# A linear-attention query stage: small softmax steps moved to GpSimd, turned halves in their own slot, and a Strassen sum moved from SBUF to PSUM

## The chip, the cores and the metric

The kernel runs on one core of a Trainium2 chip. The metric is the device time of one execution in microseconds. Three executions took 1721.21 to 1723.33 us, median 1722.93; the profile was taken in another one. The engines are called as in the profile: PE (TensorE, matmul), PEld (its weight loads), DVE (VectorE), ACT (ScalarE), POOL (GpSimd) and SP (SyncE, which issues all DMAs here).

## The reference

Two attention layers with their own inputs are computed, and their outputs stand side by side. Both have 2048 tokens, a width of 1024 and 32 heads of 32.

```python
# A: softmax attention in 4 segments of 512 tokens, with a memory carried from one to the next
q, k, v = x @ wq, x @ wk, x @ wv                  # per head
p = softmax(q k^T * scale + mask)                 # inside a segment
o = g * (phi(q) M) / (phi(q) z) + (1 - g) * p v   # then M += phi(k)^T v, z += sum phi(k)
a = o @ wo

# B: linear attention with a learned feature map per head
q, k, v = x @ wqkv
phi(t) = [softmax(t w_phi), softmax(-t w_phi)]    # 64 features a head
kv = phi(k)^T v ;  z = sum_s phi(k)
o = (phi(q) kv) / (phi(q) z + 1e-6)
b = o @ wo
return concat([a, b])
```

## The kernel before

**Products.** All large products are fp16 with split operands: a number is held as a high and a low half, and each product is three matmuls (high by high, high by low, low by high) that are summed in a PSUM bank. The products of B's tokens with their weights, and A's output product, are Strassen-Winograd products: for a pair of token tiles (256 tokens) seven half products of 12 matmuls each give four outputs of 128 tokens by 512 columns. `strassen` keeps three of the running sums in SBUF (`p1`, `u2`, `p5`, tag `cs` with four buffers). Three of its four outputs come to stand in PSUM banks (DVE adds a kept sum to a bank in place, line 620). The fourth, output (1, 1), is the sum `p5`, which DVE writes back into its SBUF buffer: `add(p5, X, p5)`. The argument `kinds` names the PSUM banks of a product. There are eight banks; the planner grants at most three of kind `proj`, three `s`, two `misc`, one `pv` and four `kv` at a time.

**Stages.** To about 900 us: A's attention, by 32 units of a segment and four heads, with the preparation of B's weights and tokens beside it. Then B's value and key products to about 1210 us: for eight token pairs, keys go through the double softmax and phi(k)^T v is summed (`kv`). Then the query stage to about 1574 us, and last A's output product.

**The query stage**, where most of the change lies, runs over 16 token tiles `c`; each even `c` makes the Strassen product of a pair. Each of the four outputs goes to `expo`: DVE takes the maxima and minima of each head (`mx`, line 1264), subtracts (`e`, lines 1266 and 1268), ACT takes the exponentials (1271), DVE sums them (1274) and takes the reciprocal (`r`, 1277). Then, for each tile and half of the heads (`hb`), 32 turns in all:

1. POOL multiplies `e` with the key sums `zb` (line 1579, two halves), DVE sums the result to `dn` (1582);
2. DVE makes the factor of each softmax, four small steps: `dn` times `r` (1585), the two sums plus 1e-6 (1587), the reciprocal (1589), and `r` times that times 2^14 (1590);
3. POOL multiplies `e` with that factor (1592);
4. ACT writes the high half (1601), DVE the low half (1603), both into a buffer `eh` that is drawn from the same ring `e` of five buffers as the softmaxes themselves;
5. SP issues a transposing DMA to `pt` (1606), PE multiplies `pt` with `kls`, phi(k)^T v (`pv`, 1615), ACT and DVE split the result into `ot` (1619, 1621), and `project` multiplies it with B's `wo` (`misc`, 396).

Beside it the weights of A's output product are made, seven Strassen forms of four blocks each (`weights`): ACT writes the high half (508), POOL the low one (509). Three forms (B11, B21, T1) stay in SBUF slots S8, S13 and S12; four go through buffers `cs` to DRAM (`wo_d`) and are loaded back into slots S0 to S3 near the end (1568).

**What sets the order.** Every step is recorded with an estimated duration and a priority, and a planner (`Graph.run`) lists them engine by engine: it takes the ready step with the earliest start, and among those the lowest priority. The order on each engine is then fixed, and on the chip each waits in its queue for the semaphores of the steps it needs. A table `MOVES` adds an offset to the priority of single jobs of an engine, by the job's number. A changed duration, engine or bank so also moves other steps.

Of the kernel before, what the change touches and what calls it, by code (L numbers as in the profile page):

```python
# [8 lines left out]
F32 = mybir.dt.float32  # L9
F32R = mybir.dt.float32r  # L10
F16 = mybir.dt.float16
# [7 lines left out]
S = 2048  # L19
# [37 lines left out]
MOVES = {  # L57
# [6 lines left out]
    "DVE": {  # L64
# [4 lines left out]
    "ACT": {  # L69
# [3 lines left out]
    "POOL": {  # L73
        59: 0.5, 67: 5.5, 70: -0.5, 93: -6, 141: 5, 154: -8, 173: 3, 199: 12, 202: -3, 211: -16.5, 234: -5.5, 238: -29.5,
        250: -2, 252: 1.5, 257: 0.5, 312: -11.5, 326: -7},
    "SP": {
        88: 5, 89: 2.5, 107: -2.5, 131: 3, 134: 21.5, 183: 8, 184: -7, 223: 6.5, 226: -9, 238: -37},
# [204 lines left out]
def tile_kernel(ctx: ExitStack, tc: tile.TileContext, ax, aw, awv, awo, beta, bx, bwqk, bwv, bphi, bwo, out):  # L282
# [10 lines left out]
    wo_d = dram.tile([4, 128, 2, 4, 512], F16, name="wo_d")  # L293
# [308 lines left out]
    def strassen(x, w, prio, kinds, tag, out):  # L602

        X, Y, Z = (bank(k, [128, 512]) for k in kinds)
# [14 lines left out]
        def add(t, ps, o):  # L619
            op(DVE, 0.62, lambda: nc.vector.tensor_tensor(o(), t(), ps(), op=OP.add), r=[t, ps], w=[o], prio=prio)  # L620

# [10 lines left out]
        add(p5, X, p5)  # L632
        out(1, 1, p5)
# [689 lines left out]
    for n, p in enumerate(VT + (0,)):  # L1323
# [9 lines left out]
        strassen(x, wvf, L + 0.5, ("proj", "proj", "proj"), ("a", [128, 512], F32, "pk", 2), vout(p, vs, L + 0.5, keep_v if p else None))  # L1333
# [36 lines left out]
    KB = ("proj", "misc", "s")  # L1370
    for at_, p in enumerate(SEQ):
# [14 lines left out]
        if at_ not in VFIRST:  # L1386
            strassen(x, wkf, P, KB if p else ("proj",) * 3, CS, kout)
# [115 lines left out]
    wform = {}  # L1503
    ast = G.buf("b", [128, 16], F32, "ast", 1)
# [20 lines left out]
    SECOND, wob = ("T2", "T3", "B22", "T4"), G.fixed(wo_d)  # L1525
# [20 lines left out]
    for c in range(NT):  # L1546
        P = Q0 + c
        if c % 2 == 0:
            sk, er = times(c // 2, 0, P - 1.2), {}

            def qout(i, hb, ps, er=er, sk=sk, P=P):
                er[i, hb] = expo(ps, P, sk)

            strassen(x, wqf, P - 1.2, ("proj", "proj", "proj"), CS, qout)
            if c + 2 < NT:
                x = x1 if c == 0 else xkept(c // 2 + 1, XS, P)
        ot = G.buf("b", [128, 2112], F16, "ot", 4)
# [16 lines left out]
        for hb in range(2):  # L1574
            e, r = er[c % 2, hb]
            dn = G.buf("b", [128, 16, 2], F32, "dn", 2)
            for a in range(2):
# [7 lines left out]
            op(DVE, 0.1, lambda dn=dn, r=r: nc.vector.tensor_tensor(dn(), dn(), r(), op=OP.mult),  # L1585
               r=[dn, r], w=[dn], prio=P)
            op(DVE, 0.1, lambda dn=dn, d1=d1: nc.vector.scalar_tensor_tensor(
                d1(), dn()[:, :, 0], 1e-6, dn()[:, :, 1], op0=OP.add, op1=OP.add), r=[dn], w=[d1], prio=P)
            op(DVE, 0.15, lambda d1=d1: nc.vector.reciprocal(d1(), d1()), r=[d1], w=[d1], prio=P)
            op(DVE, 0.1, lambda d1=d1, r=r: nc.vector.scalar_tensor_tensor(  # L1590
                r(), r(), 2.0 ** 14, d1()[:, :, None].to_broadcast([128, 16, 2]), op0=OP.mult, op1=OP.mult), r=[d1, r], w=[r], prio=P)
# [3 lines left out]
            eh = G.buf("b", [128, 16, 2, 32], F32, "e", 5)  # L1595

            def hv(eh=eh):
                return eh().rearrange("p h s d -> p (h s d)").bitcast(F16).rearrange("p (a n) -> p a n", a=2)

            for q in range(2):  # L1600
                op(ACT, 0.53, lambda q=q, e=e, hv=hv: nc.scalar.activation(  # L1601
                    hv()[:, 0, 512 * q:512 * q + 512], ev(e)[:, 512 * q:512 * q + 512], AF.Copy), r=[e], w=[(eh, (0, q))], prio=P)
                op(DVE, 0.7, lambda q=q, e=e, hv=hv: nc.vector.tensor_tensor(  # L1603
                    hv()[:, 1, 512 * q:512 * q + 512], ev(e)[:, 512 * q:512 * q + 512], hv()[:, 0, 512 * q:512 * q + 512], op=OP.subtract),
                   r=[e, (eh, (0, q))], w=[(eh, (1, q))], prio=P, port=True)
# [135 lines left out]
```

## Time and profile before

| | |
|---|---|
| median of three executions | 1722.93 us (1721.21 to 1723.33) |
| profiled execution | 1722.68 us |
| its span, first to last instruction | 1721.0 us |
| granted PE clock over the span | 0.992 |
| attention, to about 900 us | PE 887 of 900 us busy |
| values and keys, 900 to 1210 us | PE 307 of 310, DVE 245, ACT 200, POOL 182 |
| queries, 1210 to 1574 us | PE 334 of 364, DVE 334, ACT 167, POOL 212 |
| A's output, 1574 to 1721 us | PE 143 of 147, DVE 60 |

All times are of one profiled execution, in microseconds unless marked ns. A group's row has the source line, the engine, the operation, output and inputs by the program's names, their shapes and the count; behind the bar the busy time, the mean of one in ns, and behind the second bar the idle time of the engine just before them, with what ended it. A wait's row names the engine and line that waited, the work that released it, the sum, the number of times and the longest. A row of a single line has the shortest, median and longest duration in ns. Tile names come without their numbers, so `e` in a group is any buffer of that tag.

### The profile page before, as it was taken

How to read it: one execution, taken by the hardware profiler on the slowest of the kernel's cores; microseconds unless marked ns; L12 is line 12 of the kernel's file. 1: busy time of each engine (PE TensorE's matmuls, PEld its weight loads, DVE VectorE, ACT ScalarE, POOL GpSimd, SP SyncE). 2: the span in 40 equal slices, each digit the busy share in tenths (PEclk: the TensorE clock that was granted, in tenths of full speed). 3: DMA queues.
4: the chain of work that ended last, by engine and by line, in shares of the span. 5: the costliest groups of instructions: out<-in, count | busy, mean ns of one | idle time of the engine just before them, and what ended most of it. 6: DMA issues, size and time to landing. Idle time of an engine off the chain costs nothing.

```text
span 1721.0 us, 38652 instructions
## 1 busy us (share of the span) xinstructions
PE 1670.3 (97%) x14408; PEld 1002.9 (58%) x14408; DVE 1408.9 (82%) x3269; ACT 1159.6 (67%) x2131; POOL 955.2 (56%) x1184
## 2 busy tenths in 40 slices
PE   8999999999999999999999999999799899999999
PEld 6667677676776776677755545455344444444444
DVE  6999999899998767797885889778999999987441
ACT  8788999888888978678854676665445554345331
POOL 3346588653668775756742678645656767440000
PEclk9999999999999999999999999999989999999999
DMA  6556456666666573764467464566456565646311
GB/s 211 162 167 185 155 186 190 216 182 184 196 188 204 148 217 94 203 192 115 150 189 258 148 215 135 177 220 251 156 125 149 127 175 128 196 107 198 121 67 61
DMA packets 260699, 290.37 MB, mean 169 GB/s; under 512 B 138784, under 2 KB 191776, under 8 KB 253984
## 3 DMA queue, kind: packets, MB, share of 16 engines
q1 hardware_dynamic: 260512, 287.91, 55.7%
q8 instruction: 113, 1.85, 0.5%
q14 instruction: 74, 0.61, 0.1%
HBM read 160.12 MB, written 85.00 MB: 142 GB/s over the span
## 4 chain that ended last, share of the span: by engine, by line
PE 45%; DVE 15%; DMA 2%; ACT 2%; issue 1%; POOL 1%; SPq 0%; DVEq 0%; ACTq 0%; POOLq 0%
PE proj L610 14%; PE proj L396 8%; PE proj L1669 5%; PE s L610 3%; PE misc L396 3%; DVE e L1603 3%; PE s L1669 2%; DMA pt<-e 2%; PE misc L610 2%; DVE mx L1264 2%; DVE r L1274 1%; DVE dn L1582 1%; PE pv L1009 1%; PE s L973 1%; PE misc L1669 1%
## 5 line engine op out<-in xcount | busy, mean ns | idle before, releaser
L396 PE MATMUL proj<-S,S 128*128 128x128 f16 (+1 forms) x3072 | 504.6, 300 | 4.8 <-DVE S L431 1.8
L396 PEld LDWEIGHTS <-S 128*128 128x128 f16 x4608 | 329.7, 98 | 150.7 <-issue 9.3
L610 PE MATMUL proj<-S,S 128*128 128x512 f16 x1584 | 368.4, 381 | 8.3 <-ACT cs L616 6.1
L610 PEld LDWEIGHTS <-S 128*128 128x128 f16 x2016 | 191.9, 98 | 226.1 <-issue 12.8
L986 POOL TENSOR_SCALAR_AFFINE_SELECT ph<-ph 128x256 f16<-128x256 f16 (+1 forms) x448 | 194.3, 456 | 165.5 <-DVE ph L980 147.9
L878 DVE CUSTOM_DVE_ANT_0 s<-s,causal 128x256 f32<-128x256 f32 (+3 forms) x512 | 242.9, 508 | 14.1 <-PE s L872 10.8
L980 DVE SCALAR_TENSOR_TENSOR ph<-s,ph 128x512 f16<-128x512 f32 x320 | 211.0, 684 | 51.6 <-ACT ph L979 50.2
L979 ACT ACTIVATE ph<-s 128x512 f16<-128x512 f32 x320 | 191.5, 659 | 0.8
L396 PE MATMUL misc<-S,ot 128*128 128x512 f16 x768 | 172.5, 382 | 1.1 <-ACT ot L1619 1.1
L1271 ACT ACTIVATE e<-e,sk 128x256 f32<-128x256 f32 x256 | 113.8, 497 | 55.3 <-DVE e L1268 46.1
L396 PEld LDWEIGHTS <-ot 128*128 128x128 f16 x768 | 74.2, 98 | 90.8 <-issue 2.2
L1579 POOL TENSOR_TENSOR e<-e,zb 128x512 f32<-128x512 f32 x64 | 86.1, 1369 | 56.5 <-DVE r L1274 45.4
L973 PE MATMUL s<-S 104*128 104x512 f16 (+3 forms) x512 | 114.7, 299 | 0.9 <-DVE mu L951 0.5
L872 PE MATMUL s<-S 96*128 96x512 f16 (+3 forms) x512 | 113.2, 299 | 0.8 <-DVE mt L878 0.4
L977 ACT ACTIVATE s<-s,os 128x512 f32<-128x512 f32 x160 | 106.2, 714 | 9.5 <-PE s L973 6.8
L977 ACT ACTIVATE s<-s,bd 128x512 f32<-128x512 f32 x160 | 106.8, 712 | 5.5 <-PE s L973 4.8
L396 PE MATMUL proj<-wv,S 128*128 128x128 f16 x1536 | 104.9, 219 | 0.1
L1601 ACT ACTIVATE e<-e 128x512 f16<-128x512 f32 x64 | 37.3, 622 | 97.0 <-POOL e L1592 47.5
L1009 PEld LDWEIGHTS <-ph 128*128 128x128 f16 x2560 | 87.3, 96 | 17.7 <-issue 1.4
L1009 PE MATMUL pv<-vl,ph 128*128 128x66 f16 (+1 forms) x2560 | 92.2, 184 | 0.8 <-DVE h L826 0.3
L1274 DVE TENSOR_REDUCE r<-e 128x32 f32<-128x1024 f32 x64 | 76.6, 1207 | 12.5 <-ACT e L1271 12.4
L1592 POOL TENSOR_TENSOR e<-e,r 128x1024 f32<-128x1024 f32 x32 | 64.8, 2029 | 39.6 <-DVE r L1590 35.8
(342 smaller groups left out, 3355.2 us busy)
## 6 DMA issues: line engine op xcount, KB each, us to landing
S<-xf_d SPq DMA_DIRECT2D x126, 256.0 KB
S<-h SPq DMA_DIRECT2D x192, 128.0 KB
S<-wf_d SPq DMA_DIRECT2D x21, 1024.0 KB
st<-bwqk SPq DMA_DIRECT2D x64, 256.0 KB
out<-os SPq DMA_DIRECT2D x40, 256.0 KB
S<-aw SPq DMA_DIRECT2D x16, 512.0 KB
wa_d<-S SPq DMA_DIRECT2D x16, 512.0 KB
wf_d<-fo SPq DMA_DIRECT2D x32, 256.0 KB
```

The source lines that it names most:

```text
L396: op(PE, dur, lambda c=c, a=a, b=b, lv=lv, rv=rv: nc.tensor.matmul(pv(), lv(), rv(), start=(c == 0 and a + b == 0), stop=(c == n - 1 and a ...
L610: op(PE, 0.215, lambda n=n, a=a, b=b, lv=lv, rv=rv: nc.tensor.matmul(ps(), lv(), rv(), start=(start and n == 0 and a + b == 0), stop=(n == ...
L872: nc.tensor.matmul(ps()[:, o:o + 128 * i + 128], st()[0:96, 0, h, 128 * i:128 * i + 128], st()[0:96, 1, h, 0:128 * i + 128], start=True, s ...
L878: dve(0.12 + 0.00113 * n, lambda h=h, i=i, o=o, n=n: nc.vector.tensor_tensor_reduce(ps()[:, o:o + n], ps()[:, o:o + n], causal[:, 512 - n: ...
L973: nc.tensor.matmul(ps()[:, o:o + n], st()[0:104, 1, h, 128 * j:128 * j + 128], st()[0:104, 0, h, 128 * j:512], start=True, stop=True)
L977: act(0.59, lambda: nc.scalar.activation(ps(), ps(), AF.Exp, bias=0.0, scale=bdv()[:, 3, i2, 0:1]), r=[(bd, i2)], w=[ps])
L979: act(0.5, lambda: nc.scalar.activation(ph()[:, 0], ps(), AF.Copy, scale=2.0 ** 14), r=[ps], w=[(ph, 0)])
L980: dve(0.6, lambda: nc.vector.scalar_tensor_tensor(ph()[:, 1], ps(), 2.0 ** 14, ph()[:, 0], op0=OP.mult, op1=OP.subtract), r=[ps, (ph, 0)], ...
L986: nc.gpsimd.affine_select(pd, pd, pattern=[[0, n], [1, 128]], compare_op=OP.is_ge, fill=0.0, base=0, channel_multiplier=-1)
L1009: nc.tensor.matmul(ps()[:, i, n0:n1], ph()[:, a, o:o + 128], vl()[:, j, h, n0:n1], start=(i == 0 and a == 0), stop=(j == min(i, 2)), skip_ ...
L1271: op(ACT, 0.41, lambda i=i: nc.scalar.activation(e()[:, 4 * i:4 * i + 4], e()[:, 4 * i:4 * i + 4], AF.Exp, bias=0.0, scale=sk()[:, i:i + 1 ...
L1669: op(PE, 0.215, lambda n=n, a=a, b=b: nc.tensor.matmul(ps(), v(a)[:, n, :], wform[w]()[:, b, n, :], start=(start and n == 0 and a + b == 0 ...
```

## The change

**Small steps.** Of the four small DVE steps of a turn, the product with `r`, and the last product, go to POOL as they are or nearly so. The sum with 1e-6 is split: DVE sums the two numbers of a head, POOL adds 1e-6 and multiplies by 2^-14. The reciprocal stays on DVE and now gives the factor with 2^14 in it. A turn's steps so go DVE (`dn`), POOL, DVE (sum), POOL, DVE (reciprocal), POOL, POOL (`e` times the factor). In all 32 turns DVE issues 64 instructions fewer and POOL 96 more.

**Turned halves.** `eh` is one buffer in slot S13 with a place for each `hb`, and no more drawn from the ring `e`. B21 gives up S13: it goes to DRAM with the other four forms. POOL and ACT do the same 28 pairs of steps for the forms, 20 of them now into `cs` buffers instead of 16; SP issues 20 stores instead of 16 and five loads of 1 MB instead of four, into S0 to S3 and S9. The transposing DMA's planned duration on SP goes from 0.6 to 2.9 us, its landing time from 2.0 to 1.2.

**The sum.** In 24 Strassen products (3 values ahead of the pools' swap, 5 values, 8 keys, 8 queries) output (1, 1) is written by DVE into a fourth bank: `proj` for the first three, `misc` for values and keys (`proj` three times and `misc` for the first key product), `s` for the queries. Its readers then read PSUM.

**The table.** `MOVES` has other numbers. On all engines the order is the same up to about 410 us of the profile and differs from there on.

```diff
 MOVES = {
+    "DVE": {
+        43: -0.5, 70: 1, 85: -12.5, 88: -6, 93: -8, 101: -5.5, 103: 11, 106: -2, 109: 2, 114: -3.5, 118: 3.5, 129: -6, 135: -5,
...
-    wo_d = dram.tile([4, 128, 2, 4, 512], F16, name="wo_d")
+    wo_d = dram.tile([5, 128, 2, 4, 512], F16, name="wo_d")
...
-        X, Y, Z = (bank(k, [128, 512]) for k in kinds)
+        X, Y, Z = (bank(k, [128, 512]) for k in kinds[:3])
...
             op(DVE, 0.62, lambda: nc.vector.tensor_tensor(o(), t(), ps(), op=OP.add), r=[t, ps], w=[o], prio=prio)
+            return o
...
         mult(X, 4)
-        add(p5, X, p5)
-        out(1, 1, p5)
+        out(1, 1, add(p5, X, bank(kinds[3], [128, 512])))
...
-        strassen(x, wvf, L + 0.5, ("proj", "proj", "proj"), ("a", [128, 512], F32, "pk", 2), vout(p, vs, L + 0.5, keep_v if p else None))
+        strassen(x, wvf, L + 0.5, ("proj", "proj", "proj", "proj"), ("a", [128, 512], F32, "pk", 2), vout(p, vs, L + 0.5, keep_v if p else None))
...
-    KB = ("proj", "misc", "s")
+    KB = ("proj", "misc", "s", "misc")
...
-            strassen(x, wkf, P, KB if p else ("proj",) * 3, CS, kout)
+            strassen(x, wkf, P, KB if p else ("proj",) * 3 + ("misc",), CS, kout)
...
+    eh = G.buf("slot", [128, 2, 2048], F16, "S13")
...
-    SECOND, wob = ("T2", "T3", "B22", "T4"), G.fixed(wo_d)
+    SECOND, wob = ("B21", "T2", "T3", "B22", "T4"), G.fixed(wo_d)
...
-            strassen(x, wqf, P - 1.2, ("proj", "proj", "proj"), CS, qout)
+            strassen(x, wqf, P - 1.2, ("proj", "proj", "proj", "s"), CS, qout)
...
-            for f, i in (("B11", 8), ("B21", 13), ("T1", 12)):
+            for f, i in (("B11", 8), ("T1", 12)):
...
-                wform[f] = G.buf("slot", [128, 2, 4, 512], F16, f"S{i}")
+                wform[f] = G.buf("slot", [128, 2, 4, 512], F16, f"S{VS[i]}")
...
-            op(DVE, 0.1, lambda dn=dn, r=r: nc.vector.tensor_tensor(dn(), dn(), r(), op=OP.mult),
+            op(POOL, 0.25, lambda dn=dn, r=r: nc.gpsimd.tensor_tensor(dn(), dn(), r(), op=OP.mult),
                r=[dn, r], w=[dn], prio=P)
-            op(DVE, 0.1, lambda dn=dn, d1=d1: nc.vector.scalar_tensor_tensor(
-                d1(), dn()[:, :, 0], 1e-6, dn()[:, :, 1], op0=OP.add, op1=OP.add), r=[dn], w=[d1], prio=P)
+            op(DVE, 0.12, lambda dn=dn, d1=d1: nc.vector.tensor_reduce(d1(), dn(), axis=AX.X, op=OP.add), r=[dn], w=[d1], prio=P)
+            op(POOL, 0.25, lambda d1=d1: nc.gpsimd.tensor_scalar(d1(), d1(), 1e-6, 2.0 ** -14, op0=OP.add, op1=OP.mult), r=[d1], w=[d1], prio=P)
             op(DVE, 0.15, lambda d1=d1: nc.vector.reciprocal(d1(), d1()), r=[d1], w=[d1], prio=P)
-            op(DVE, 0.1, lambda d1=d1, r=r: nc.vector.scalar_tensor_tensor(
-                r(), r(), 2.0 ** 14, d1()[:, :, None].to_broadcast([128, 16, 2]), op0=OP.mult, op1=OP.mult), r=[d1, r], w=[r], prio=P)
+            op(POOL, 0.25, lambda d1=d1, r=r: nc.gpsimd.tensor_tensor(
+                r(), r(), d1()[:, :, None].to_broadcast([128, 16, 2]), op=OP.mult), r=[d1, r], w=[r], prio=P)
...
-            eh = G.buf("b", [128, 16, 2, 32], F32, "e", 5)
-
-            def hv(eh=eh):
-                return eh().rearrange("p h s d -> p (h s d)").bitcast(F16).rearrange("p (a n) -> p a n", a=2)
+            def hv(hb=hb):
+                return eh()[:, hb].rearrange("p (a n) -> p a n", a=2)
...
-            op(SP, 0.6, lambda pt=pt, hv=hv: nc.sync.dma_start_transpose(
+            op(SP, 2.9, lambda pt=pt, hv=hv: nc.sync.dma_start_transpose(
                 pt().rearrange("p a g t -> p (a g) t"), hv().rearrange("p a n -> p (a n)")),
-               r=[(eh, (a, q)) for a in range(2) for q in range(2)], w=[pt], prio=P, lat=2.0, kb=512)
+               r=[(eh, (hb, a, q)) for a in range(2) for q in range(2)], w=[pt], prio=P, lat=1.2, kb=64)
```

DVE's order in the query stage before, around the fifth of the 32 turns. The turn's own rows are the second of its two sums `dn_19849`, the product with `r_19784`, the sum `d1_19929`, the reciprocal and the last product. Between them stand steps of the next pair's softmax (`mx`, `e`, `r`) and the low halves `ot` of earlier turns. Numbers tell buffers of one name apart.

```order
L1264 TENSOR_REDUCE mx_19856<-proj_19497 128x16 x2
L1582 TENSOR_REDUCE dn_19849<-e_19719 128x16
L1266 TENSOR_TENSOR e_19896<-proj_19497,mx_19856 128x16x32
L1585 TENSOR_TENSOR dn_19849<-dn_19849,r_19784 128x32
L1621 SCALAR_TENSOR_TENSOR ot_19892<-pv_19858,ot_19892 128x512
L1587 SCALAR_TENSOR_TENSOR d1_19929<-dn_19849 128x16
L1274 TENSOR_REDUCE r_19931<-e_19827 128x32
L1274 TENSOR_REDUCE r_19940<-e_19793 128x32
L1589 RECIPROCAL d1_19929<-d1_19929 128x16
L1277 RECIPROCAL r_19940<-r_19940 128x32
L1590 SCALAR_TENSOR_TENSOR r_19784<-r_19784,d1_19929 128x32
```

The rows L1585, L1587 and L1590 are the ones that the change takes from DVE.

The same turn after, with the changed file's lines (two or three lower): the second sum `dn_19806`, then `d1_19862` from `dn_19806` and its reciprocal. L1600 is the subtraction that was L1603.

```order
L1618 SCALAR_TENSOR_TENSOR ot_19800<-pv_19768,ot_19800 128x512
L1262 TENSOR_REDUCE mx_19819<-proj_19522 128x16 x2
L1581 TENSOR_REDUCE dn_19806<-e_19683 128x16
L1266 TENSOR_TENSOR e_19855<-mx_19819,proj_19522 128x16x32
L1618 SCALAR_TENSOR_TENSOR ot_19800<-pv_19825,ot_19800 128x512
L1586 TENSOR_REDUCE d1_19862<-dn_19806 128x16
L1272 TENSOR_REDUCE r_19864<-e_19795 128x32
L1275 RECIPROCAL r_19864<-r_19864 128x32
L1588 RECIPROCAL d1_19862<-d1_19862 128x16
L1600 TENSOR_TENSOR S13_19672<-e_19499,S13_19672 128x512 x2
L1600 TENSOR_TENSOR S13_19672<-e_19427,S13_19672 128x512 x2
```

The products L1585 and L1590 are gone from DVE, the sum L1586 is one reduction, and ahead of it and behind it DVE has to have POOL's answer.

POOL's order at the same turn, before: steps of the output weights (`S12`, `h3`), then the two products of this turn with the key sums, one of the next turn's, and the multiplication with the factor.

```order
L509 TENSOR_TENSOR S12_19693<-h3_17196,S12_19693 128x512
L501 TENSOR_TENSOR h3_17196<-h3_17216,h3_17196 128x512
L1579 TENSOR_TENSOR e_19719<-e_19719,zb_19387 128x512 x2
L1579 TENSOR_TENSOR e_19793<-e_19793,zb_19387 128x512
L1592 TENSOR_TENSOR e_19719<-e_19719,r_19784 128x1024
```

Between a turn's product with the key sums and its multiplication with the factor POOL has one other step.

And after, where L1591 is the multiplication with the factor (1592 before), L1584, L1587 and L1589 are the new small steps, and L507 and L1578 what was L509 and L1579:

```order
L1589 TENSOR_TENSOR r_19524<-r_19524,d1_19744 128x32
L1591 TENSOR_TENSOR e_19499<-e_19499,r_19607 128x1024
L1584 TENSOR_TENSOR dn_19806<-dn_19806,r_19747 128x32
L1591 TENSOR_TENSOR e_19427<-e_19427,r_19524 128x1024
L1587 TENSOR_SCALAR d1_19862<-d1_19862 128x16
L507 TENSOR_TENSOR S12_19793<-h3_17153,S12_19793 128x512
L1589 TENSOR_TENSOR r_19747<-r_19747,d1_19862 128x32
L1578 TENSOR_TENSOR e_19795<-e_19795,zb_19462 128x512
L1591 TENSOR_TENSOR e_19683<-e_19683,r_19747 128x1024
```

The turn's first small step (`dn_19806`) stands between the multiplications of two other turns, the second (`d1_19862`) behind the second of them, and its last (`r_19747`) behind a low half of the output weights.

More of the change, by code (lines that the diff above doesn't have):

```diff
@@ L57 @@
 MOVES = {
[6 rows of a table removed]
-    "DVE": {
[4 rows of a table removed]
-    "ACT": {
[3 rows of a table removed]
+    "DVE": {
[3 rows of a table added]
+    "ACT": {
[9 rows of a table added]
     "POOL": {
-        59: 0.5, 67: 5.5, 70: -0.5, 93: -6, 141: 5, 154: -8, 173: 3, 199: 12, 202: -3, 211: -16.5, 234: -5.5, 238: -29.5,
-        250: -2, 252: 1.5, 257: 0.5, 312: -11.5, 326: -7},
+        67: 17, 70: -1, 93: -6, 131: -0.5, 141: 1, 148: -7.5, 199: 13.5, 217: -4, 238: -38, 245: 0.5, 250: -4.5, 312: -5},
     "SP": {
-        88: 5, 89: 2.5, 107: -2.5, 131: 3, 134: 21.5, 183: 8, 184: -7, 223: 6.5, 226: -9, 238: -37},
+        88: 5.5, 89: 3.5, 134: 33.5, 149: -3.5, 226: -19.5},
 }
@@ L1594, in tile_kernel @@
             pt = G.buf("b", [128, 2, 8, 128], F16, "pt", 3)
[L1595 to L1598 removed]
+            def hv(hb=hb):
+                return eh()[:, hb].rearrange("p (a n) -> p a n", a=2)
             for q in range(2):
                 op(ACT, 0.53, lambda q=q, e=e, hv=hv: nc.scalar.activation(
[L1602 removed]
+                    hv()[:, 0, 512 * q:512 * q + 512], ev(e)[:, 512 * q:512 * q + 512], AF.Copy), r=[e], w=[(eh, (hb, 0, q))], prio=P)
                 op(DVE, 0.7, lambda q=q, e=e, hv=hv: nc.vector.tensor_tensor(
                     hv()[:, 1, 512 * q:512 * q + 512], ev(e)[:, 512 * q:512 * q + 512], hv()[:, 0, 512 * q:512 * q + 512], op=OP.subtract),
[L1605 to L1606 removed]
+                   r=[e, (eh, (hb, 0, q))], w=[(eh, (hb, 1, q))], prio=P, port=True)
+            op(SP, 2.9, lambda pt=pt, hv=hv: nc.sync.dma_start_transpose(
                 pt().rearrange("p a g t -> p (a g) t"), hv().rearrange("p a n -> p (a n)")),
[L1608 removed]
+               r=[(eh, (hb, a, q)) for a in range(2) for q in range(2)], w=[pt], prio=P, lat=1.2, kb=64)
             pn = bank("pv", [128, 4, 128])
```

22 rows, old and new, of the table MOVES are left out of this document.

## The prediction

> **What bounds the kernel now.** I read first the page's table of engines, then the table by stretches of time, to see in which stage an engine is short. The columns of the second are the stretch, its length, and the busy time of each engine with its instructions.
>
> ```profile
> PE 1670.3 (97%) x14408; PEld 1002.9 (58%) x14408; DVE 1408.9 (82%) x3269; ACT 1159.6 (67%) x2131; POOL 955.2 (56%) x1184
> core 0: us, PE busy (x) PEld busy (x) DVE busy (x) ACT busy (x) POOL busy (x), PEclk, DMA share, GB/s
> 0.00:410.00 410.00, 397.80 (x4185) 282.71 (x4186) 361.49 (x1028) 356.41 (x633) 239.06 (x384) 0.99 0.60 184
> 410.00:900.00 490.00, 488.78 (x5228) 340.95 (x5227) 407.67 (x1194) 386.05 (x691) 321.92 (x475) 1.00 0.59 172
> 900.00:1210.00 310.00, 307.33 (x2169) 155.97 (x2169) 245.13 (x432) 199.67 (x409) 181.91 (x180) 1.00 0.59 199
> 1210.00:1574.00 364.00, 333.51 (x2172) 158.70 (x2171) 334.29 (x531) 166.74 (x323) 212.29 (x145) 0.97 0.59 154
> ```
>
> Over the whole span PE is the bound: it idles 51 us of 1721. But 30.5 of them (364 less 333.5) lie in the query stage, 1210 to 1574, and only there is DVE as busy as PE. In the 800 us ahead of it PE idles 3.9 us, so nothing can be won there. So the next question is what PE waits for in the query stage, from the list of waits, and how the worst of them looks in PE's timeline.
>
> ```profile
> PE pv L1615 <- DMA pt<-e: 21.3, 8, 11.0
> 1213.42 10.52 PE L610 MATMUL proj<-S,S 128*128 128x512 f16 x48
> 1247.06 1.49 PE L1615 MATMUL pv<-pt,kls 128*64 128x128 f16 x24 [11.04 <-DMA pt<-e]
> 1251.61 5.28 PE L610 MATMUL proj<-S,S 128*128 128x512 f16 x12 [3.06 <-ACT cs L616]
> ```
>
> PE waits eight times for the transposing DMA, 11 us of it at the stage's start, where the last instruction ahead of the DMA is DVE's subtraction L1603. Each wait has a second price: twelve products of L610 took 5.28 us right after it, where 48 took 10.52 before (2.63 for twelve), and the granted clock of the stage is 0.97. So at most 30.5 us and some 4 us of slow products (2.65 in this row, and a like amount after the other waits) can be won, 34.5 in all. DVE feeds the DMA, so I look at what DVE does in this stretch, by shapes.
>
> ```profile
> L1603 DVE TENSOR_TENSOR e<-e x64: 674/947/2446, 1239.6 to 1548.6; 128x512 f16<-128x512 f32 x64
> L1603 DVE TENSOR_TENSOR e<-e 128x512 f16<-128x512 f32 x64 | 75.9, 1221 | 12.4 <-ACT e L1601 12.2
> L1585 DVE TENSOR_TENSOR dn<-dn,r 128x32 f32<-128x32 f32 x32 | 21.6, 676 | 0.3
> L1587 DVE SCALAR_TENSOR_TENSOR d<-dn 128x16 f32<-128x16 f32 x32 | 12.0, 385 | 0.2
> L1590 DVE SCALAR_TENSOR_TENSOR r<-r,d 128x32 f32<-128x32 f32 x32 | 10.1, 326 | 0.2
> L1589 DVE RECIPROCAL d<-d 128x16 f32<-128x16 f32 x32 | 7.3, 237 | 0.3
> L1590 DVE SCALAR_TENSOR_TENSOR r<-r,d x32: 121/191/1906, 1229.9 to 1542.3; 128x32 f32<-128x32 f32 x32
> 1369.16 1.91 DVE L1590 SCALAR_TENSOR_TENSOR r<-r,d 128x32 f32<-128x32 f32 x1
> 1369.11 1.91 POOL L1592 TENSOR_TENSOR e<-e,r 128x1024 f32<-128x1024 f32 x1 [1.40 <-DVE r L1590]
> ```
>
> A step on 32 numbers a partition takes 121 ns at best and up to 1906, and the last two rows show when: it lies beside a POOL multiplication to the hundredth of a microsecond. DVE is not computing there; it is held while POOL works in SBUF. The same stretch stands in L1603, 674 ns at best and 1221 on the mean.
>
> **The change, term by term** (in DVE time of the query stage, then in PE time).
>
> *Small steps to POOL.* DVE loses L1585, L1587 and L1590: 21.6 + 12.0 + 10.1 = 43.7 us. It gains 32 sums of 128x16 from 128x32, which it has not run. Bounds: 0.13 us (about the best small step) and 0.67 (L1585's mean), 4 to 21 us; I take 0.237, the reciprocal on the same 16 numbers, which has one SBUF input as the sum has and is not stretched: 7.6. Net -36.1.
>
> *The sum in a PSUM bank.* Of four outputs of each Strassen product one lay in SBUF (`cs`); now all lie in PSUM.
>
> ```profile
> L1266 DVE TENSOR_TENSOR e<-cs,mx 128x512 f32<-128x512 f32 x8 | 9.8, 1220 | 0.0
> L1268 DVE TENSOR_TENSOR e<-mx,cs 128x512 f32<-128x512 f32 x8 | 9.7, 1216 | 0.1
> L1266 DVE TENSOR_TENSOR e<-proj,mx 128x512 f32<-128x512 f32 x23 | 15.4, 674 | 0.0
> L1268 DVE TENSOR_TENSOR e<-mx,proj 128x512 f32<-128x512 f32 x23 | 15.5, 672 | 2.5 <-DMA pt<-e 2.4
> L1264 DVE TENSOR_REDUCE mx<-cs 128x16 f32<-128x512 f32 x14 | 9.3, 676 | 0.1
> L1264 DVE TENSOR_REDUCE mx<-proj 128x16 f32<-128x512 f32 x46 | 29.7, 677 | 0.2
> ```
>
> The two subtractions get shorter by 546 and 544 ns, eight each: -8.7. The maxima cost the same from both places, so they give nothing. The Trainium skill's page "VectorE: DVE Perf Modes" (section Rules for kernel authors) says the opposite of this edit: for many steps on a product, copy it from PSUM to SBUF first. By that rule the term would be no gain, and, as an estimate, the sum below some 5 us worse; the equal maxima and the shorter subtractions above are against it here.
>
> The price is the bank: it is held for the four reads, 4 x 0.67 = 2.7 us, in eight products of the key stage too, where it is the second of two `misc` banks. If PE waited for it each time, 22 us; if the next product always found another bank, 0. I take 0: the other three outputs hold their banks through the same four reads, and PE idles 2.7 us in all of 900 to 1210.
>
> *What POOL gains.* 96 small steps. Nearest rows, from the attention stage and this one:
>
> ```profile
> L1030 POOL TENSOR_TENSOR rd<-rd,sc 128x16 f32<-128x16 f32 x32 | 8.2, 257 | 15.8 <-DVE rd L1029 13.2 <-DVE pst L534 1.0 <-DVE bd L742 0.9
> L1276 POOL TENSOR_SCALAR r<-r 128x32 f32<-128x32 f32 x32 | 10.0, 315 | 43.2 <-DVE r L1274 37.2 <-DVE big L551 3.1 <-DVE wsc L411 2.8
> L1247 POOL TENSOR_SCALAR sk<-swf,pst 128x4 f32<-128x4 f32 x5 | 4.0, 806 | 4.3 <-ACT e L1271 4.3
> ```
>
> Two of three at 315 (32 numbers), one at 257 (16): 28.4 us, between 25 (all 257) and 77 (all 806); I take the rows with equal shapes. POOL goes from 212 to 241 of 364, so its own time is covered. But more POOL work holds L1603 longer: its stretch, 64 x 547 ns = 35 us at 212 us of POOL, grows by 28.4/212, +4.7 us. The Trainium skill's "GPSIMD Engine Reference" (section 3.1) has GpSimd about twice as slow as VectorE on elementwise steps with two inputs; on 43.7 us that is an estimate of 87 us more on POOL, +14 for L1603 instead of 4.7, and a sum about 5 us worse. The rows give 257 to 315 ns against the 676 that DVE really spends here, so I go by the rows.
>
> *New waits.* Each turn now passes DVE, POOL, DVE, POOL, DVE, POOL: DVE's sum and reciprocal each wait for a POOL step, and behind them in DVE's queue stand the next maxima, subtractions and evictions. 64 new places. Low end: the attention stage has the same sequence, reciprocal, POOL product, DVE product, with POOL busy 322 of 490 us.
>
> ```profile
>   POOL rd L1030: 1.1, 4
> POOL e L1592 <- DVE r L1590: 35.8, 25, 4.3
> ```
>
> The first row is what DVE waits there in 32 turns, 0.03 us each, 2 us for 64. High end: POOL's own wait for the small steps, 35.8/25 = 1.43 us each, 92 us. I take 0.15 each, 10 us, since the low row is the same sequence under the same planner with a POOL that is even fuller.
>
> *Halves in slot S13.* This frees the ring `e`: four buffers are drawn a pair instead of eight, out of five.
>
> ```profile
> ACT e L1601 <- DMA pt<-e: 14.6, 4, 4.7
> ```
>
> That wait loses its cause at most places: the slot's half was last read one token tile earlier. ACT is busy 167 of 364, so I count nothing directly; bounds 0 and -14.6.
>
> *B21 through DRAM.* Four more stores and one more 1 MB load at the end of the stage.
>
> ```profile
> 1481.45 8.09 SPq L1568 DMA_DIRECT2D S<-wo_d  x4
> L1669 PE MATMUL proj<-S,ot x192: 379/379/379, 1561.3 to 1706.2; 128*128 128x512 f16 x192
> ```
>
> A load is 2 us of SP's queue; one transpose behind it starts 2 us later. The forms are first used at 1561, 70 us after their loads are issued, and that gap covers it: 0, with +2 as the other end.
>
> *The other engines' order.* The order of all engines is rewritten from about 410 us on. PE idles 3.9 us from there to 1210; I put +2 on it, between -3.9 and the rival below.
>
> Sum on DVE: 334.3 - 36.1 - 8.7 + 4.7 + 10 = 304 us, 30 less, so the stage is PE's. PE's 30.5 us of idle time split at 1260:
>
> ```profile
> 1210.00:1260.00 50.00, 34.50 (x204) 17.11 (x203) 47.13 (x82) 20.89 (x43) 28.66 (x20) 0.83 0.56 164
> 1210.00:1260.00 50.00, 2.55 (x4) 0.83 0.56 164
> 1210.00:1260.00 50.00, 2.99 (x4) 0.83 0.56 164
> 1210.00:1260.00 50.00, 0.71 (x4) 0.83 0.56 164
> ```
>
> The first row is all engines, the other three L1585, L1587 and L1590 on DVE. In this stretch PE idles 15.5 us and DVE gives up 6.2 of 47: I take 6 off, since the chain sum, POOL, subtraction, DMA to the first `pv` stays. Of the other 15.0, where DVE gives up 37.5 of its small steps in 314 us, I take two thirds, 10; late next is the DMA itself. With half of the 4 us of slow products: -6 - 10 - 2 + 2 = -16. The profiled execution took 1722.68 us, 1.7 over its span, against a median of 1722.93; so I forecast 1707.
>
> **Rivals.** *All idle time goes* (chance 0.07): DVE 304 of 330 leaves PE alone; 1722.9 - 34.5 = 1688. Against it: the start of the stage is a chain, not a load.
>
> *POOL's queue holds DVE* (0.20, slower). The relief without new waits is 36.1 + 8.7 - 4.7 = 40.1 us; shared by 64 places it is used up at 0.63 us each, and from there the stage is longer. A small step that finds a POOL multiplication half done (half of L1592's 1.91) and then runs 0.3 waits 1.25; if three places in four are so, 60 us, and 1722.9 + 20 = 1743. For it: in the order after, a turn's small steps stand behind multiplications of other turns and halves of weights. Against it: the 1.1 us of the attention stage.
>
> *The new order costs more than the stage gains* (0.15, slower). In the first 410 us PE idles 12.2, 3%; were the 800 us that follow to become like that, +24 - 4, and with -14 from the queries 1729. Against it: DVE and POOL have reserves of 80 us and more in both stretches.
>
> *The gaps stay* (0.11): `pv` waits for the DMA, and if its latency and the now longer round trip, not DVE's load, set them, the relief only becomes DVE idle time; 1722.
>
> **How the numbers follow.** The forecast has 0.47, on its own 1694 to 1716. Faster by over 0.2% (3.4 us, about what a measurement can tell from no change) are the forecast, the first rival and 0.01 of the last: 0.55. Within 0.2%: 0.09 of the last. Slower: 0.20 + 0.15 + 0.01 = 0.36. The range runs from 1690 to 1735; half of the first rival's chance and the upper part of the second lie outside.
>
> **What would show it.** Right: DVE busy in the query stage falls to about 300 us, the POOL steps take about 0.3 us, `e` no longer reads from `cs`, DVE waits for POOL at its sum and reciprocal come to 10 us, and PE's waits for `pt` shrink. Wrong: those waits on DVE pass 40 us; L1603's mean rises well over 1.3 us; or PE idles more between 410 and 1210, for `misc` or `proj` banks above all.

## The result, and the profile after

The changed kernel takes 1697.67 us (median of four executions, 1695.04 to 1699.23) against 1722.73 us: a ratio of 0.985, 95% interval 0.984 to 0.987, 25 us faster. The forecast was 1707, within 1690 to 1735. The profiled execution took 1699.08 us over a span of 1697.4, so its rows stand for the median to 1.4 us.

First the table of engines and the table by stretches. The stages are cut where they end now: the last product of the key stage is at 1214 (1210 before), the last product of the query stage, `ot` with B's `wo`, at 1548 (1574).

```profile
PE 1668.2 (98%) x14408; PEld 1002.5 (59%) x14408; DVE 1354.2 (80%) x3205; ACT 1158.9 (68%) x2131; POOL 965.4 (57%) x1280
...
0.00:1214.00 1214.00, 1197.03 (x11586) 781.78 (x11587) 1011.04 (x2652) 940.09 (x1731) 736.33 (x1040) 0.99 0.60 183
1214.00:1264.00 50.00, 45.11 (x293) 21.91 (x291) 48.46 (x84) 24.81 (x52) 35.67 (x37) 1.00 0.57 164
1264.00:1548.00 284.00, 280.65 (x1871) 133.07 (x1866) 235.74 (x385) 143.77 (x273) 193.41 (x204) 1.00 0.69 174
1548.00:1697.40 149.40, 145.40 (x674) 65.77 (x672) 58.95 (x86) 50.25 (x76) 0.00 (x0) 1.00 0.24 85
```

PE's idle and busy time account for the whole gain. Before, PE idled 16.1 us up to 1210, 30.5 in the query stage and 4.1 behind it, 50.7 in all; now it idles 17.0, 8.2 (50 - 45.11 + 284 - 280.65) and 4.0, together 29.2. That is 21.5 less, and PE is busy for 2.1 us less (1670.3 to 1668.2): 23.6, the difference of the two spans. DVE is busy for 284.2 us of the 334 of this stage, 85%, where it was 334.3 of 364, 92%.

Then what PE waits for (1210 to 1574), and its timeline up to the first `pv`:

```profile
PE pv L1612 <- DMA pt<-S: 3.0, 3, 1.5
PE proj L608 <- ACT cs L614: 2.4, 3, 1.1
PE misc L394 <- DVE ot L1618: 1.8, 1, 1.8
...
1217.94 3.62 PE L608 MATMUL proj<-S,S 128*128 128x512 f16 x16
1222.24 18.29 PE L608 MATMUL proj<-S,S 128*128 128x512 f16 x84 [0.69 <-ACT cs L614]
1241.17 2.75 PE L608 MATMUL proj<-S,S 128*128 128x512 f16 x12 [0.63 <-ACT cs L614]
1245.45 0.86 PE L1612 MATMUL pv<-pt,kls 128*64 128x128 f16 x24 [1.53 <-DMA pt<-S]
```

The waits for the transposing DMA have fallen from 21.3 us to 3.0. The first `pv` is hardly earlier, 1245.45 for 1247.06, but PE fills the time ahead of it with Strassen products, and the hole of 11 us has shrunk to 1.5. Last DVE and POOL in the query stage, by shapes:

```profile
L1600 DVE TENSOR_TENSOR S<-e,S 128x512 f16<-128x512 f32 x64 | 65.8, 1078 | 3.1 <-ACT S L1598 2.9
L1586 DVE TENSOR_REDUCE d<-dn 128x16 f32<-128x32 f32 x32 | 5.1, 166 | 5.7 <-POOL dn L1584 5.6
L1588 DVE RECIPROCAL d<-d 128x16 f32<-128x16 f32 x32 | 7.3, 237 | 1.2 <-POOL d L1587 1.1
L1264 DVE TENSOR_TENSOR e<-s,mx 128x512 f32<-128x512 f32 x8 | 5.4, 672 | 0.0
L1266 DVE TENSOR_TENSOR e<-mx,s 128x512 f32<-128x512 f32 x8 | 5.3, 668 | 0.0
L1584 POOL TENSOR_TENSOR dn<-dn,r 128x32 f32<-128x32 f32 x32 | 8.8, 277 | 7.8 <-DVE dn L1581 7.4
L1587 POOL TENSOR_SCALAR d<-d 128x16 f32<-128x16 f32 x32 | 8.8, 276 | 8.5 <-DVE d L1586 6.4
L1589 POOL TENSOR_TENSOR r<-r,d 128x32 f32<-128x32 f32 x32 | 9.9, 316 | 8.4 <-DVE d L1588 4.6 <-DVE d L1586 3.7
```

Where DVE spent 43.7 us on three small steps, it spends 5.1 on one, and POOL 27.5 on three. The two subtractions that read the fourth output of a Strassen product are short from the bank (672 and 668 ns for 1220 and 1216).

### The profile page after: what moved, and what is told of

The parts are those of the page before. It is cut to its first block, busy times and chain, and to the rows that moved or that the text cites. A ratio compares the mean times of both kernels' runs of the same rounds, so it can differ in the third digit from the quotient of the medians.

```text
span 1697.4 us, 38668 instructions
## 1 busy us (share of the span) xinstructions
PE 1668.2 (98%) x14408; PEld 1002.5 (59%) x14408; DVE 1354.2 (80%) x3205; ACT 1158.9 (68%) x2131; POOL 965.4 (57%) x1280
## 4 chain that ended last, share of the span: by engine, by line
PE 45%; DVE 5%; DMA 1%; ACT 0%; issue 0%; SPq 0%; DVEq 0%; ACTq 0%
PE proj L608 17%; PE misc L394 8%; PE proj L1666 5%; PE s L608 4%; PE s L1666 2%; PE misc L608 2%; PE kv L1423 1%; PE misc L1666 1%; PE pv L1612 1%; DVE S L1600 1%; PE proj L394 1%; DVE mx L1262 1%; DVE r L1272 1%; DVE dn L1581 1%; PE pv L1007 1%; PE s L971 1%
## 5 line engine op out<-in xcount | busy, mean ns | idle before, releaser
L608 PE MATMUL proj<-S,S 128*128 128x512 f16 x1584 | 364.6, 379 | 2.4 <-ACT cs L614 2.4
L876 DVE CUSTOM_DVE_ANT_0 s<-s,causal 128x512 f32<-128x512 f32 (+3 forms) x512 | 242.9, 509 | 15.2 <-PE s L870 11.5
L1578 POOL TENSOR_TENSOR e<-e,zb 128x512 f32<-128x512 f32 x64 | 87.2, 1376 | 30.4 <-DVE r L1272 25.6
L1007 PEld LDWEIGHTS <-ph 128*128 128x128 f16 x2560 | 87.1, 96 | 15.5 <-issue 0.8
L876 DVE DVE_READ_ACCUMULATOR2_ANT mt<- 128x1 f32 x512 | 72.4, 141 | 0.0
L1011 DVE TENSOR_REDUCE oall<-pv 128x132 f32<-128x264 f32 x128 | 54.5, 426 | 19.1 <-PE pv L1007 18.5
```

Source lines behind the costliest of these rows:

```text
L608: op(PE, 0.215, lambda n=n, a=a, b=b, lv=lv, rv=rv: nc.tensor.matmul(ps(), lv(), rv(), start=(start and n == 0 and a + b == 0), stop=(n == ...
L876: dve(0.12 + 0.00113 * n, lambda h=h, i=i, o=o, n=n: nc.vector.tensor_tensor_reduce(ps()[:, o:o + n], ps()[:, o:o + n], causal[:, 512 - n: ...
L1007: nc.tensor.matmul(ps()[:, i, n0:n1], ph()[:, a, o:o + 128], vl()[:, j, h, n0:n1], start=(i == 0 and a == 0), stop=(j == min(i, 2)), skip_ ...
```

## The experiments

Theory: before the change, DVE sets the pace of the query stage, and it loses that time in small steps that are held while POOL works in SBUF; taking them away is most of the gain (the theory of the load). Rivals: the new order (the table of moves) is the gain; the bank is; the slot is; or POOL's queue or the chain to the DMA sets the pace, and the relief of DVE buys little. All ratios are against the kernel before, run beside the experiment.

**1. The kernel before without two of its small steps, order kept.**

```diff
-op(DVE, 0.1, lambda dn=dn, r=r: nc.vector.tensor_tensor(dn(), dn(), r(), op=OP.mult),
+op(DVE, 0.1, lambda dn=dn, r=r: None,
...
-op(DVE, 0.1, lambda d1=d1, r=r: nc.vector.scalar_tensor_tensor(r(), r(), 2.0 ** 14, ...
+op(DVE, 0.1, lambda d1=d1, r=r: None, r=[d1, r], w=[r], prio=P)
```

> The kernel before in its own order on every engine, with two of DVE's four small steps of each turn left out (the product of dn with r, L1585, and the last product with the factor, L1590), so the query rows are not normalised as they should be. Theory 'held small steps' (DVE's small two-input steps are held beside POOL's work, DVE then hands the halves to the transposing DMA late, and PE waits): 31.7 us of DVE time go, PE's idle time in the query stage falls from 30 us to about 10, and the time from 1722.7 to 1697 to 1707. Rival 'order' (the new order of the engines is what gains): at most 5 us, 1718 or more. Rival 'round trip' (PE waits for the latency of the chain POOL, DVE, POOL, DMA, not for DVE's load): 2 steps of 0.12 us out of the chain, at most 5 us.

Measured: 1707.5 us, ratio 0.990 (0.988 to 0.992): 16 us without any other order, just beyond the slow end of what the theory gave. The row of the small step that stayed, in the query stage:

```profile
L1587 DVE SCALAR_TENSOR_TENSOR d<-dn 128x16 f32<-128x16 f32 x32 | 27.8, 878 | 0.2
```

It took 385 ns before. The hold has passed to the next small step with two inputs, which now begins while a POOL instruction runs 28 times of 32 (10 before): of the 31.7 us that the two steps took, 15.8 came back there, and so not 31.7 us of DVE time went, as the theory had it, but half. The hole of 11 us ahead of the first `pv` stayed (11.1).

**2. The changed kernel without POOL's two small products, order kept.**

```diff
-op(POOL, 0.25, lambda dn=dn, r=r: nc.gpsimd.tensor_tensor(dn(), dn(), r(), op=OP.mult),
+op(POOL, 0.25, lambda dn=dn, r=r: None,
...
-op(POOL, 0.25, lambda d1=d1, r=r: nc.gpsimd.tensor_tensor(r(), r(), d1()..., op=OP.mult), r=[d1, r], w=[r], prio=P)
+op(POOL, 0.25, lambda d1=d1, r=r: None, r=[d1, r], w=[r], prio=P)
```

> The kernel after in its own order, with the same two steps left out, which are now POOL's (L1584 and L1589; the query rows are again not normalised). 18.7 us of POOL time go. Theory 'held small steps': POOL is not what PE waits for, so 0 to 3 us, 1695 to 1698. Rival 'POOL's queue': the longer round trip now sets what idle time PE still has (8.7 us in the query stage), so most of that goes, 1690 or less.

Measured: 1700.3 us, ratio 0.986 (0.985 to 0.988), no gain over the changed kernel. DVE's wait at its sum falls from 5.7 us to 0.1, and the time does not follow: what POOL's queue costs DVE here is no limit.

```profile
L1586 DVE TENSOR_REDUCE d<-dn 128x16 f32<-128x32 f32 x32 | 4.9, 161 | 0.1
```

**3. The changed kernel with its value, key and query sums back in SBUF (21 of the 24 products), order kept.**

```diff
-        out(1, 1, add(p5, X, bank(kinds[3], [128, 512])))
+        o5 = bank(kinds[3], [128, 512])
+        if tag[0] == "b":
+            o5.make = p5
+        out(1, 1, add(p5, X, o5))
```

> The kernel after in its own order, but output (1, 1) of the 21 Strassen products of values, keys and queries in that pool is written back to SBUF as before; the fourth bank is planned and left unused. Theory 'held small steps': the two subtractions cost DVE about 0.5 us more each, 8.7 us in the query stage, and DVE now has 40 us to spare there: 0 to +4 us, 1698 to 1702. Rival 'bank': the sum in PSUM carries a good part of the gain, +8 us or more.

Measured: 1703.8 us, ratio 0.989 (0.987 to 0.990), 6 us behind the changed kernel: more than the theory's 0 to +4, less than the rival's +8. The two subtractions, in the query stage:

```profile
L1267 DVE TENSOR_TENSOR e<-cs,mx 128x512 f32<-128x512 f32 x8 | 8.7, 1084 | 0.0
L1269 DVE TENSOR_TENSOR e<-mx,cs 128x512 f32<-128x512 f32 x8 | 13.6, 1705 | 0.0
```

They take 22.3 us for 10.7. How much of that reaches the time is not shown, since the value and key products were edited too. The stretches of this run:

```profile
0.00:1214.00 1214.00, 1192.69 (x11595) 779.55 (x11596) 1017.38 (x2653) 940.37 (x1731) 742.47 (x1040) 1.00 0.60 183
1214.00:1264.00 50.00, 44.15 (x266) 20.61 (x265) 48.46 (x84) 24.25 (x51) 35.72 (x37) 1.00 0.55 157
1264.00:1555.00 291.00, 285.42 (x1888) 135.01 (x1889) 247.96 (x387) 145.66 (x277) 196.51 (x204) 0.99 0.67 170
```

PE idles 11.4 us in the query stage (8.2 in the changed kernel) and 21.3 ahead of it (17.0), and is busy for 3 us less in all: the larger part of what was added lies ahead of the query stage.

**4. The new table of moves on the kernel before**, `MOVES` alone exchanged, the instructions those of before.

> The kernel before with the other table of offsets alone. Theory 'held small steps': no gain, since the steps on DVE are the same and the numbers were made for another program: 1720 to 1745. Rival 'order': a good part of the 25 us, 1712 or less.

Measured: 1711.4 us, ratio 0.993 (0.991 to 0.994). The theory of the load had expected nothing, and was wrong here by 12 us: an order alone moves this stage. The three small steps are hardly shorter in sum (40.8 us for 43.7), and PE's waits for `pt` fall from 21.3 to 11.3 us.

**5. The old table on the changed kernel.**

> The kernel after with the table of offsets of the kernel before. Theory 'held small steps': the steps are off DVE whatever the table, so PE's idle time behind 1260 us (15 before, 3.3 after) stays under 7; the start of the stage may fall back to 15 us of idle time: 1700 to 1712. Theory 'order' (the table carries the gain, as the table alone gave 11 to 12 us): 1715 or more.

Measured: 1698.4 us, ratio 0.987 (0.985 to 0.988), no difference that can be measured from the changed kernel, and a little better than the theory's 1700 to 1712. So the changed kernel's gain does not need its table.

**6. Only the small steps moved to POOL** (the diff of L1585, L1587 and L1590), the old table.

> The kernel before with the small steps on GpSimd alone (old table, halves in the ring e, sum in SBUF). Theory 'held small steps': about what leaving two of them out gave, 1703 to 1713, with DVE's subtraction L1603 at 1.1 us. Theory 'order': the order was made for the other program, so nothing or a loss, 1720 or more. Rival 'POOL's queue': DVE waits for POOL at the sum and the reciprocal for 20 us and more.

Measured: 1703.9 us, ratio 0.990 (0.988 to 0.991), 18 of the 25 us. DVE waits for POOL at the sum and the reciprocal for 8.2 us, not for the rival's 20.

**7. Only the slot**: the halves in S13, B21 by way of DRAM, and the planner's new duration of the transposing DMA.

> The kernel before with the turned halves in slot S13, B21 through DRAM and the other planned duration of the transposing DMA alone (old table, small steps on DVE). Theory 'held small steps': DVE's work is the same, so 1715 to 1728. Rival 'ring' (the freed buffers let the next softmax and PE's products run ahead, and that closes the gap at the start of the query stage): the first gap falls from 11 us to under 5, and the time to 1712 or less.

Measured: 1720.5 us, ratio 0.999 (0.997 to 1.000): 2 us.

**8. The changed kernel with its small steps back on DVE.**

> The kernel after with the small steps back on DVE (new table, slot and fourth bank kept). Theory 'held small steps': DVE is at 330 us again and most of PE's idle time behind 1260 us comes back: 1707 to 1720. Theory 'order': slot, bank and table hold the gain, 1702 or less.

Measured: 1720.9 us, ratio 0.999 (0.998 to 1.000). The steps took 629, 391 and 273 ns, 40.8 us, and the whole gain was gone. That is more than the 18 of run 6; the plan was made anew here, so part of it may be the order. The next run keeps the order.

**9. The three small steps on DVE in a form with one input, order of before.** Two of them only copy, so the rows are not normalised.

```diff
-nc.vector.tensor_tensor(dn(), dn(), r(), op=OP.mult)
+nc.vector.tensor_reduce(dn(), dn()[:, :, :, None], axis=AX.X, op=OP.add)
-nc.vector.scalar_tensor_tensor(d1(), dn()[:, :, 0], 1e-6, dn()[:, :, 1], op0=OP.add, op1=OP.add)
+nc.vector.tensor_reduce(d1(), dn(), axis=AX.X, op=OP.add)
-nc.vector.scalar_tensor_tensor(r(), r(), 2.0 ** 14, d1()..., op0=OP.mult, op1=OP.mult)
+nc.vector.tensor_reduce(r(), r()[:, :, :, None], axis=AX.X, op=OP.add)
```

> The order of before is kept and the three small steps stay on DVE, but each is put as a TENSOR_REDUCE with one operand: two of them over an axis of length one, so that nothing is multiplied (the sums aren't multiplied by `r`, and `r` isn't multiplied by `d`: the rows are not normalised); the third as the changed kernel has it. Theory that DVE is held at a step that reads two operands from SBUF while POOL works: none of the three is held, each takes about 0.17 us as the sum in the changed kernel (0.166), so 96 x 0.17 = 16 us stand for 43.7; the hold doesn't pass to the long products either, since those were 1221 ns before and 1094 with two of the steps gone. 28 us less on DVE by the price that the move to POOL had (18 us gained for 36) is 14: 1705 to 1711 us. Rival, that the step right behind a released POOL waits whatever its form: the first of them stays at 0.65 us or more and the time above 1715 us.

Measured: 1702.9 us, ratio 0.989 (0.987 to 0.991), 20 us, 2 us better than the expected range. The query stage on DVE:

```profile
L1601 DVE TENSOR_TENSOR e<-e 128x512 f16<-128x512 f32 x64 | 77.6, 1249 | 13.8 <-ACT e L1599 13.5
L1585 DVE TENSOR_REDUCE dn<-dn 128x32 f32<-128x32 f32 x32 | 5.5, 175 | 0.3
L1587 DVE TENSOR_REDUCE d<-dn 128x16 f32<-128x32 f32 x32 | 5.3, 174 | 0.2
L1589 DVE TENSOR_REDUCE r<-r 128x32 f32<-128x32 f32 x32 | 4.5, 152 | 0.0
```

As many steps, at the same places, beside the same POOL: 15.3 us for 43.7. None is held, and the long subtraction has taken up none of it but 1.7 us. This is the cleanest proof of the cause: neither order, bank, slot nor POOL's part differ from before. The single instructions of the two traces show the same. Before, 36 of the 96 small steps began while a POOL instruction ran that had 0.25 us or more to go; all 36 ended within 0.15 us of that instruction's end (0.39 to 1.91 us), and the other 60 took 0.12 to 0.19. Here 55 of 96 began so, and none took over 0.19 us.

The Trainium skill's page "SBUF — State Buffer" (section Who interferes with whom) states the rule: a VectorE instruction with two SBUF inputs contends with a GpSimd instruction that reads SBUF, and the order of issue decides which of the two is blocked; one with a single input doesn't contend, outside the modes that use both of VectorE's ports, and a reduction never does on this chip. The rows agree: 676 ns with two inputs, 175 with one.

**10. The kernel before, the planner told the true durations**: 0.10 us made 0.68, 0.39 and 0.33 in the three lines.

> The kernel before with the planner's durations of the three small steps raised from 0.10 to what the trace has (0.68, 0.39 and 0.33 us); the instructions are the same, the order of the query stage is planned anew, the table of moves is the old one. Theory that the held time itself is what costs: DVE still has its 44 us of small steps, only their places are better known: no more than the 11 us that the other table gave to the same instructions, 1712 to 1722 us. Rival, that the plan built on 0.10 us was the loss (the small steps on POOL helped because POOL's durations are planned rightly): most of the 18 us, 1703 to 1709 us.

Measured: 1734.5 us, ratio 1.007 (1.005 to 1.009). Both expectations missed: it is 12 us slower. The waits of PE (1205 to 1590), and four groups of DVE:

```profile
PE pv L1615 <- DMA pt<-e: 34.4, 9, 14.9
...
L1603 DVE TENSOR_TENSOR e<-e 128x512 f16<-128x512 f32 x64 | 65.7, 1069 | 12.9 <-ACT e L1601 12.9
L1587 DVE SCALAR_TENSOR_TENSOR d<-dn 128x16 f32<-128x16 f32 x32 | 18.4, 581 | 0.1
L1585 DVE TENSOR_TENSOR dn<-dn,r 128x32 f32<-128x32 f32 x32 | 18.0, 569 | 0.1
L1590 DVE SCALAR_TENSOR_TENSOR r<-r,d 128x32 f32<-128x32 f32 x32 | 17.0, 533 | 0.1
```

The hold is spread otherwise, 53.4 us in place of 43.7, and PE waits 13 us longer for `pt`. The theory that a wrong planned duration was the loss falls: the measured durations don't help. The step is not long, it is held, and where it meets POOL changes with the plan.

**11. The changed kernel without the bank, planned anew.**

```diff
-        out(1, 1, add(p5, X, bank(kinds[3], [128, 512])))
+        add(p5, X, p5)
+        out(1, 1, p5)
```

> The changed kernel with the sum back in SBUF in all stages and no fourth bank taken, planned anew (with the sum sent to SBUF in the unchanged order it took 1703.8). Theory that the sum in a bank is worth about 5 us by its shorter readers (548 ns each for 16 steps, and what waits for them): 1702 to 1705 us. Rival, that the bank's worth was the unfitted order of that run and a new plan gets it back: 1697 to 1700 us. Rival, that taking the bank lengthens the earlier stages by 4 us, which a kernel without it saves: the last `kv` product ends near 1210 us in place of 1214.

Measured: 1724.6 us, ratio 1.002 (1.001 to 1.003). Both forecasts of the time missed by some 20 us. The sign of the third came, the last `kv` product ends at 1210.3; but run 5 takes the bank and ends there too (1210.5), so the bank did not set it, and it saved nothing here. In PE's timeline:

```profile
1517.26 10.52 PE L394 MATMUL misc<-S,ot 128*128 128x512 f16 x48
1545.64 1.49 PE L1613 MATMUL pv<-pt,kls 128*64 128x128 f16 x24 [17.86 <-DMA pt<-S]
1551.20 1.49 PE L1613 MATMUL pv<-pt,kls 128*64 128x128 f16 x24 [4.07 <-DMA pt<-S]
```

In this plan the last query product ends at 1517 us (1471 in the changed kernel), and no product is left to cover the softmax behind it: 17.9 us of idle time in one place, 28 in all at `pv`. Run 3 has its sums in SBUF as well (but for three value products) and took 1703.8 by the order of the changed kernel, so the order is worth about 21 us here, as much as the held steps. A theory of load cannot price that.

**12. The changed kernel with a sum of two inputs**, order kept.

```diff
-nc.vector.tensor_reduce(d1(), dn(), axis=AX.X, op=OP.add)
+nc.vector.tensor_tensor(d1(), dn()[:, :, 0], dn()[:, :, 1], op=OP.add)
```

> The changed kernel in its own order, with one instruction of another form: the sum of a row's two halves on DVE is a TENSOR_TENSOR that adds the two columns, both read from SBUF, in place of the TENSOR_REDUCE of one operand (0.166 us). The result is the same. The two POOL steps around it stay on POOL, which goes on with a step of 1.3 to 1.9 us as soon as it has delivered `dn`. Theory that DVE is held at a step with two operands from SBUF while POOL works: this step takes 0.6 to 0.9 us (0.878 where it was the first such step of the chain), 14 to 23 us more on DVE; at 0.6 to 0.7 us of time for each (18 for 28, 20 for 28) the time is 1706 to 1714 us. Rival, that the changed kernel has DVE time to spare by now (DVE waits for others at several places): the step is held, but the time stays at 1697 to 1701 us. Rival, that the hold was a matter of the place right behind the reduction and not of the form: the step takes under 0.3 us, and the time is that of the changed kernel.

Measured: 1699.7 us, ratio 0.986 (0.985 to 0.988): no difference that can be measured from the changed kernel.

```profile
L1600 DVE TENSOR_TENSOR S<-e,S 128x512 f16<-128x512 f32 x64 | 60.5, 994 | 2.4 <-ACT S L1598 2.4
L1586 DVE TENSOR_TENSOR d<-dn 128x16 f32<-128x16 f32 x32 | 19.8, 627 | 5.0 <-POOL dn L1584 5.0
```

The step is held as soon as it reads two inputs, 627 ns for 166, so the form is the cause in this order too. But 5.3 of its 14.7 us come off the long subtraction (65.8 to 60.5), and the rest is absorbed. The first rival was right: after the change DVE has time to spare.

**Where this leaves the theories.** In unchanged orders, the held steps are worth 20 us on the kernel before (run 9), and the bank 6 on the changed one (run 3): 1722.9 to 1702.9, and 1703.8 to 1697.7, 26 against 25 measured. That is one path and no sum of parts, since the parts' worth depends on the kernel: the table gave 12 us to the kernel before (run 4) and nothing to the changed one (run 5), and a held step cost the changed kernel nothing that could be measured (run 12). The slot by itself gave 2 (run 7). What stays open is how much of the gain of run 6 and of the loss of runs 8 and 11 is load and how much is the plan that each got; only runs 1, 2, 3, 9 and 12 keep an order. The bank on the kernel before, and the changed kernel without the slot, were not tried.

## Why the prediction was right

The sign, the mechanism of the held steps and the range held; it was 9 us too cautious, and the way from DVE's relief to PE's idle time was in part luck, as the terms show.

- *Small steps, -36.1 on DVE.* Measured -38.6 (43.7 to 5.1). The sum took 166 ns for the assumed 237: the reciprocal has one input as well, but takes longer, 237 ns in both kernels.
- *Sum in a bank, -8.7.* Measured -8.8 (19.5 to 10.7), worth 6 us of time by run 3, ahead of the query stage as well as in it. The length of these subtractions is the hold again, which the prediction did not say: of the 16 that read `cs` before, the eight that began beside a POOL instruction took up to 2.29 us and the others 0.68 to 0.69; from PSUM 46 of 62 began so after the change, and none took over 0.69. The Trainium skill's page "VectorE: DVE Perf Modes" (section Rules for kernel authors) leaves the choice, for elementwise steps on a product, to read PSUM as it is or, for many steps, to copy it to SBUF first. The second does not hold here: run 3, which reads the sum from SBUF, is the slower one.
- *Longer stretch of L1603, +4.7.* Wrong in its sign: the group fell from 75.9 to 65.8 us although POOL is busier. The step that failed is the scaling by POOL's total time. The same instructions as before in another order had a mean of 1069 ns (run 10) for 1221. The stretch goes by which DVE step happens to meet a POOL step, not by how much POOL works: 36 of the 64 began beside a POOL instruction before, 29 after, 22 in run 10. I have no rule to forecast it.
- *POOL +28.4.* Measured 27.5. (The row at 315 ns, L1276, is of the key stage, and not of the attention or the query stage as the prediction had it.)
- *New waits 10 us.* Measured 6.7 (5.6 at the sum, 1.1 at the reciprocal). So the rival with POOL's queue fell, and run 2 shows that nothing is gained by taking the first of these waits away.
- *DVE 304.* Measured 284.2 busy and 6.7 of those waits, 291. Most of the 13 us of difference is L1603's, 14.8 below what was put down. So the forecast set 16 us of PE's idle time against 30 of relief on DVE, and 22.3 against 43 were measured: the price was right, but a third of the relief came from a group whose sign was forecast wrong, and that is luck.
- *PE: the stage's start -6, the rest -10.* Measured -10.6 (15.5 to 4.9) and -11.7 (15.0 to 3.3). The term that failed most is the first one. Run 9, with DVE's relief alone, left 11.2 us (its row for 1210 to 1260 follows), so the relief is worth 4.3 of it, below the 6. The other 6 are not relief: the first `pv` is only 1.6 us earlier, and PE has more products ahead of it. The prediction looked at the chain to `pv` and did not ask what else PE could do meanwhile. The runs narrow down what lets the plan do that. In the first 50 us behind the last `kv` product PE idles 4.7 to 7.0 us in all kernels with both the slot and the small products off DVE (the changed one and runs 2, 3, 5, 11, 12), and 11.2 to 16.5 in all that lack one of the two (the kernel before and runs 1, 4 and 6 to 10). So neither the table nor the bank is needed for it, and the slot, which counted for 0 in the forecast, has a part; how it does it isn't shown.

```profile
1210.00:1260.00 50.00, 38.81 (x253) 19.49 (x252) 46.73 (x90) 23.34 (x48) 28.51 (x20) 0.86 0.59 169
```

- *Slow products -2.* PE's busy time fell by 2.1 us, and the granted clock at the stage's start is 1.00 in place of 0.83.
- *Other stages +2.* PE's idle time ahead of the query stage rose by 0.9.
- *Slot and fifth load 0.* Run 7: -2, with an interval that nearly touches none.

Of the rivals, "the new order costs more" had the wrong sign in this kernel, but runs 10 and 11 show that an order can cost 12 and 21 us. "All idle goes", at 1688, lies as near to the measured 1698 as the forecast: 22.3 of the 30.5 us went. With that "the gaps stay" fell.

## What to carry to other kernels

A tiny step on DVE that reads two SBUF operands beside a busy POOL should be priced at what POOL's running instruction has left, not at its own size; put it in a form with one input or give it to POOL itself. For a long step, an operand in PSUM ended the hold (the subtractions); that wasn't tried on a small one. Leaving one such step out moves the hold to the next one in the chain (run 1), so all of them have to go. And where a planner sets the order, compare an edit in the old order first: a new plan alone moved this kernel by 12 us down and 21 up.

## What had not been expected of the hardware

- The hold is inherited: with two of the held steps gone, the mean of the third rose from 385 to 878 ns, with no change of its own. With all three reduced to one input it took 174 (run 9).
- A small step takes POOL longer (276 to 316 ns) than a DVE that is not held (152 to 175), and still less than the 676, 385 and 326 ns that DVE spent beside a busy POOL.
- What a microsecond of DVE is worth depends on how full it is: 28 us taken off the kernel before gave 20 us of time (run 9), 9 us put back on the changed kernel (14.7 less 5.3, run 12) cost nothing that could be measured.
